# Gated linear attention with a cosine-gated feed-forward behind it: 256-token units, a second product that is held back, decay groups of two chunks, and elementwise products on GpSimd

## The chip, the cores and the metric

The kernel runs on one core of one Trainium2 chip. The metric is the time of one execution on the device in microseconds. The kernel before was timed in three runs: median 227.28 us (226.5 to 227.76). One execution was profiled; it took 227.1 us, of which the trace spans 225.3 us from the first to the last instruction.

## The reference, cut to what matters

There are 4 sequences of 768 tokens with 8 heads of 48 channels. The first stage is a gated linear recurrence for each head; its output, laid out as 3072 tokens of 384 channels, goes into a feed-forward stage with two products.

```
f = 1 / (1 + exp(-f_logit))
for t in range(768):
    state = f[:, :, t, :, None] * state + k[:, :, t] (outer) v[:, :, t]
    y[:, :, t] = q[:, :, t] @ state
x = y.transpose(0, 2, 1, 3).reshape(3072, 384)
h = x @ w_in            # 384 x 2048
out = (h * cos(h)) @ w_out   # 2048 x 384
```

Inputs and the output are float32. Matmul operands are bfloat16 in the kernel.

## The kernel before, in words

**Attention by chunks.** Each sequence is cut into 6 chunks of 128 tokens, so there are 24 chunks, numbered 0 to 23 here. `chunk_load` brings f, v, k and q of a chunk (192 KB each) on the SP queue; six sets of load buffers rotate. `decay_group` (L313 on) takes a group of chunks: on ScalarE exp and ln of f (L328, L331) give the log decay, TensorE sums it over the tokens with a triangular matrix (L343, L346), and ScalarE makes exp of the sum and of its negative (L353: `b` and `bi`). `attend` then multiplies q by `b` and k by `bi` (L365 and L368, `qtd` and `ktd`, each on VectorE or GpSimd), GpSimd casts v (L371, `vz`), TensorE transposes both (L383), ScalarE or VectorE copies the result from PSUM (L397 or L399, `qdt` and `kz`), TensorE forms the scores (L414), VectorE masks them (L419, `am`), TensorE forms the output of the chunk (L481 from the scores, L485 from the state), and ScalarE or VectorE casts it to `xT` (L496 or L498). Beside this the state goes on from chunk to chunk: L434 on TensorE, L445 on VectorE (`st`), L453 on GpSimd (`sz`).

**Feed-forward by units.** `moe(t0, T)` takes a unit of T tokens: four units of 128 and then five of 512. The first product (L516) fills a PSUM bank of 512 columns at a time (a tile); ScalarE takes the cosine of it (L523), VectorE multiplies the two into `gT` (L527; `gc` in the small units). The second product (L537) is issued in steps of four matmuls, sixteen for 128 tokens; the result is copied (L546 or L548) and stored by the SP queue (L551). There are 8 PSUM banks; the tiles of the first product hold at most 4, and both products together at most 5.

**Two sets of function tables.** exp and ln are in one table set of ScalarE and the cosine (computed as a sine) is in another. Going from one to the other costs an ACT_TABLE_LOAD (L582 for exp and ln, L523 for the sine). Copies and casts need neither. From the first exp of a decay group to its last, ScalarE takes no cosine.

**What sets the order.** All instructions are first written down as operations with a cost, an engine or a choice of engines, a priority `prio` and their inputs and outputs. `Plan.run` then sets them one by one: of all operations whose inputs are set it takes the one that can start first by the costs, and of those with the same start the one with the lowest `prio`. The resulting order is fixed; on the chip each engine works through its own list and waits where an input or a buffer is not there. For attention `prio` is the chunk number; for the feed-forward it is 2.0 plus the first chunk of the unit plus a part for the tile. `GROUPS` gives the sizes of the decay groups: 1, 1, 1, 1, 2, and then six times 3.

Of the kernel before, what the change touches and what calls it, by code (L numbers as in the profile page):

```python
# [207 lines left out]
def kernel(  # L208
# [11 lines left out]
    B, H, S, D = q.shape  # L220
    C = 128
# [5 lines left out]
    KF = d_ff // 128  # L227
    TOK = 512
    NT = n_tokens // TOK
    GROUPS = [1, 1, 1, 1, 2] + [3] * 6  # L230
    LEAD = 2.0

    cpool = ctx.enter_context(tc.tile_pool(name="const", bufs=1))
    ppool = ctx.enter_context(tc.tile_pool(name="psum", bufs=1, space=bass.MemoryType.PSUM))
# [6 lines left out]
    def slots(name, n, shape, dt=BF16, zero=None):  # L241
        aps = []
        for i in range(n):
            t = cpool.tile(shape, dt, name=f"{name}_{i}")
            if zero is not None:
                zero.memset(t, 0.0)
            aps.append(t)
        return Slots(aps, name)
# [20 lines left out]
    szS = slots("sz", 3, [128, NP, SW], zero=nc.vector)  # L269
    stS = slots("st", 2, [128, NP, 2 * D], F32)  # L270
    x_sb = [cpool.tile([128, KM, TOK], BF16, name=f"xT_{i}") for i in range(NT)]
    gS = slots("gT", 2, [128, KF, TOK])
    gcS = slots("gc", 4, [128, KF, C])
    coS = slots("cosh", 4, [128, TOK])
    otS = slots("ot", 4, [128, d_model], F32)
    base = banks("ps", 8)
# [8 lines left out]
    P = Plan()  # L285
# [7 lines left out]
    def load_weights(part, i, prio):  # L293
# [3 lines left out]
        else:  # L297
# [7 lines left out]
    xT = [Val(ap=x_sb[n * C // TOK][:, :, n * C % TOK:n * C % TOK + C])  # L305
          for n in range(n_tokens // C)]
# [13 lines left out]
    def decay_group(chunks, g, prio):  # L320

        outs = []
        for (b, c, ld) in chunks:
# [8 lines left out]

            e1 = P.op({"ACT": 515.0}, act1, reads=[f], writes=[f], prio=prio, table="E", grp=g)
            P.op({"ACT": 515.0}, act2, reads=[f], writes=[sp], prio=prio, table="E", grp=g)
            for (_, _, ld2) in chunks:
# [3 lines left out]
        for (b, c, ld, sp) in outs:  # L339
# [12 lines left out]
            def ex(e, pc=pc, o=bt, s=-1.0, n=H * D + NP):  # L352
                nc.scalar.activation(out=o.ap, in_=pc.ap[:, 0:n], func=AF.Exp, scale=s)  # L353

            P.op({"ACT": 400.0}, ex, reads=[pc], writes=[bt], prio=prio, table="E", grp=g)
            P.op({"ACT": 400.0}, lambda e, pc=pc, bi=bi, ex=ex: ex(e, pc, bi, 1.0, H * D),
                 reads=[pc], writes=[bi], prio=prio, table="E", grp=g)
            res.append((b, c, ld, bt, bi))
        return res

    def attend(b, c, ld, bt, bi, prio):
        _, vf, kf, qf = ld
        qtd, ktd, vz = Val(qtdS), Val(ktdS), Val(vzS)
        E = lambda e: nc.vector if e == "DVE" else nc.gpsimd
        P.op({"POOL": 1000.0, "DVE": 560.0}, lambda e: E(e).tensor_mul(  # L365
            out=qtd.ap[:, :, 0:D], in0=qf.ap,
            in1=bt.ap[:, 0:H * D].rearrange("p (h d) -> p h d", d=D)), reads=[qf, bt], writes=[qtd], prio=prio)
        P.op({"POOL": 1000.0, "DVE": 560.0}, lambda e: E(e).tensor_mul(  # L368
            out=ktd.ap[:, :, 0:D], in0=kf.ap,
            in1=bi.ap.rearrange("p (h d) -> p h d", d=D)), reads=[kf, bi], writes=[ktd], prio=prio)  # L370
        o = P.op({"POOL": 510.0}, lambda e: nc.gpsimd.tensor_copy(  # L371
# [114 lines left out]
                                     rhs=qdt.ap[:, n, :], **fl)  # L486
        rd = [vz, qdt] + ams + ([S_in] if S_in is not None else [])
        P.op({"PE": len(jobs) * N128}, pey, reads=rd, writes=[py], prio=prio, lat=170.0)
        tok = b * S + c * C
        x = xT[tok // C]  # L490

        def yev(e):
# [9 lines left out]
    def moe(t0, T):  # L502

        n0 = t0 // C
        xs, gT = xT[n0:(t0 + T) // C], Val(gS if T == TOK else gcS)
        x = x_sb[t0 // TOK][:, :, t0 % TOK:t0 % TOK + T]
        G = 512 // T
        span = T / C
        for j in range(KF // G):
            ph, co = Val(phS), Val(coS)  # L510

            def g1(e, j=j, ph=ph):
                for g in range(G):
                    f0 = (j * G + g) * 128
                    for m in range(KM):
                        nc.tensor.matmul(ph.ap[:, g * T:(g + 1) * T],  # L516
                                         lhsT=w_in_bf[:, m, f0:f0 + 128], rhs=x[:, m, :],
                                         start=(g == 0 and m == 0),
                                         stop=(g == G - 1 and m == KM - 1))
            pr = LEAD + n0 + 0.5 * span * j * G / KF  # L520
            P.op({"PE": G * 3 * (T / 2.4 + 2.0)}, g1, reads=xs + [w_in_v[j * G // 4]],
                 writes=[ph], prio=pr, lat=170.0)
            P.op({"ACT": 640.0}, lambda e, ph=ph, co=co: nc.scalar.activation(  # L523
                out=co.ap, in_=ph.ap, func=AF.Sin, bias=halfpi),
                reads=[ph], writes=[co], prio=pr, table="S")
            gv = gT.part(lambda a, j=j: a[:, j * G:(j + 1) * G, 0:T])
            P.op({"DVE": 650.0}, lambda e, ph=ph, co=co, gv=gv: nc.vector.tensor_mul(  # L527
                out=gv.ap, in0=ph.ap.rearrange("p (g t) -> p g t", t=T),
                in1=co.ap.rearrange("p (g t) -> p g t", t=T)),
                reads=[ph, co], writes=[gv], prio=pr)  # L530
        for i in range(T // 128):
            po, ot = Val(poS), Val(otS)
            pr = LEAD + n0 + 0.5 * span + 0.5 * i
            for s in range(4):
                def g2(e, i=i, s=s, po=po):
                    for j in range(4 * s, 4 * s + 4):
                        nc.tensor.matmul(po.ap[:, 0:d_model],  # L537
                                         lhsT=gT.ap[:, j, i * 128:(i + 1) * 128],
                                         rhs=w_out_bf[:, j, :], start=(j == 0), stop=(j == KF - 1))
                P.op({"PE": 4 * 162.5}, g2,  # L540
                     reads=[gT.parts[q] for q in range(4 * s // G, (4 * s + 3) // G + 1)] + [w_out_v[s]],
                     writes=[po], prio=pr, lat=170.0 if s == 3 else 0.0)

            def ev(e, po=po, ot=ot):
                if e == "ACT":
                    nc.scalar.copy(out=ot.ap, in_=po.ap[:, 0:d_model])  # L546
                else:
                    nc.vector.tensor_copy(out=ot.ap, in_=po.ap[:, 0:d_model])  # L548
            P.op({"ACT": 380.0, "DVE": 530.0}, ev, reads=[po], writes=[ot], prio=pr)
            r0 = t0 + i * 128  # L550
            P.op({"SP": 500.0}, lambda e, ot=ot, r0=r0: nc.sync.dma_start(  # L551
                out=out[r0:r0 + 128, :], in_=ot.ap), reads=[ot], prio=pr, lat=2000.0)
# [2 lines left out]
    nc.vector.memset(halfpi, HALF_PI)  # L555

    chunks = [(b, c) for b in range(B) for c in range(NCH)]
    units = [C] * (TOK // C) + [TOK] * (NT - 1)
    n, t0 = 0, 0
    for g, size in enumerate(GROUPS):  # L560
        grp = []
        for j, (b, c) in enumerate(chunks[n:n + size]):
            grp.append((b, c, chunk_load(b, c, float(n + j))))
        for j, item in enumerate(decay_group(grp, g, float(n))):
            attend(*item, prio=float(n + j))
            if n + j == 0:
                for i in range(NW):
                    load_weights(0, i, 0.2 + 0.1 * i)
                for i in range(KF // 4):
                    load_weights(1, i, 1.2 + 0.5 * i)  # L570
        n += size
        while units and t0 + units[0] <= n * C:
            moe(t0, units[0])
            t0 += units.pop(0)
# [40 lines left out]
```

## Time and profile before

| | us |
|---|---|
| median of 3 runs (lowest, highest) | 227.28 (226.5, 227.76) |
| the profiled execution | 227.1 |
| its span in the trace | 225.3 |
| TensorE (PE) busy | 192.8 (86%) |
| ScalarE (ACT) busy | 159.6 (71%) |
| VectorE (DVE) busy | 151.1 (67%) |
| GpSimd (POOL) busy | 52.3 (23%) |
| mean granted TensorE clock | 0.975 |

Busy time is the time in which at least one instruction of the engine was under way; the end of a matmul is modelled, so a row of matmuls is best priced by the distance between starts. The chain of waits is followed back from the last instruction; its rows give a start, a duration and what was under way, and "issue" is time in which nothing that the profile shows was waited for. PEld is the loading of weights, which overlaps matmuls. HBM transfers use 1.0 of the DMA engines' time up to about 120 us, when the last inputs have come, and little after it.

### The profile page before, as it was taken

What the parts mean: (1) busy time and instruction counts of PE and PEld (TensorE: products, weight loads), DVE (VectorE), ACT (ScalarE), POOL (GpSimd) and SP (SyncE); (2) the same over time, 40 slices, a digit from 0 to 9 for tenths busy, and PEclk for the clock granted to TensorE, in tenths of its full rate; (3) what the DMA queues carried; (4) which work ended last, traced back from release to release, by engine and by line L of the source; (5) the groups of instructions that cost most, each with busy time, mean ns of one, the idle gap of its engine ahead of it and who ended that gap; (6) DMA issues with size and microseconds to landing.
All of it is one profiled execution on the core that took longest, in us unless ns stands there. A gap on an engine that the chain in (4) does not pass through costs nothing.

```text
span 225.3 us, 4647 instructions
## 1 busy us (share of the span) xinstructions
PE 192.8 (86%) x1760; PEld 128.2 (57%) x1760; DVE 151.1 (67%) x269; ACT 159.6 (71%) x283; POOL 52.3 (23%) x86
## 2 busy tenths in 40 slices
PE   0076788998579889999969999999999999889994
PEld 0056466877369445676743567645676456654562
DVE  7854647788396499449997934998069971449800
ACT  4237559999886999748695984999569962449721
POOL 3800503212034430118380030600038000300000
PEclk9999999999967999999996999999999999999998
DMA  6999998999999999498999212000110001100011
GB/s 137 185 187 185 172 193 186 198 205 204 193 206 212 183 225 186 115 214 168 207 210 210 40 70 73 0 0 3 70 73 3 0 3 70 70 3 0 0 70 70
DMA packets 107030, 27.03 MB, mean 120 GB/s; under 512 B 100353, under 2 KB 107009, under 8 KB 107009
## 3 DMA queue, kind: packets, MB, share of 16 engines
q1 hardware_dynamic: 103296, 23.60, 49.7%
q0 software_dynamic: 3712, 3.15, 8.8%
q8 instruction: 13, 0.21, 0.4%
q14 instruction: 9, 0.07, 0.1%
HBM read 25.17 MB, written 4.72 MB: 133 GB/s over the span
## 4 chain that ended last, share of the span: by engine, by line
PE 66%; DVE 13%; ACT 10%; issue 6%; POOL 2%; DVEq 0%; POOLq 0%
PE ps L537 26%; PE ps L516 25%; PE ps L481 5%; PE ps L414 4%; PE ps L383 3%; ACT kz L397 3%; DVE am L419 2%; PE ps L485 2%; DVE ktd L368 2%; DVE qtd L365 1%; DVE gc L527 1%; ACT L523 1%; ACT bi L353 1%; ACT b L353 1%; ACT xT L496 1%
## 5 line engine op out<-in xcount | busy, mean ns | idle before, releaser
L516 PE MATMUL ps<-xT,w_in_bf 128*128 128x512 bf16 (+1 forms) x432 | 67.8, 316 | 3.0 <-ACT xT L496 1.4
L523 ACT ACTIVATE cosh<-ps,halfpi 128x512 bf16<-128x512 f32 x96 | 60.2, 697 | 4.1 <-PE ps L516 4.0
L537 PE MATMUL ps<-w_out_bf,gT 128*128 128x384 bf16 x320 | 53.6, 326 | 0.0
L516 PEld LDWEIGHTS <-w_in_bf 128*128 128x128 bf16 x432 | 35.7, 101 | 31.3 <-issue 5.9
L527 DVE TENSOR_TENSOR gT<-ps,cosh 128x512 bf16<-128x512 f32 x80 | 50.1, 686 | 4.7 <-ACT cosh L523 4.7
L419 DVE TENSOR_TENSOR am<-ps,umask 128x512 bf16<-128x512 f32 x48 | 30.6, 684 | 27.2 <-PE ps L414 26.4
L537 PEld LDWEIGHTS <-gT 128*128 128x128 bf16 x320 | 31.1, 98 | 20.6
L453 POOL TENSOR_TENSOR sz<-st,b 64x192 bf16<-64x192 f32 x32 | 16.6, 519 | 83.4 <-DVE st L445 78.7
L546 ACT COPY ot<-ps 128x384 f32<-128x384 f32 x17 | 8.2, 479 | 24.5 <-PE ps L537 24.5
L371 POOL CAST vz<-v 128x384 bf16<-128x384 f32 x24 | 13.5, 563 | 47.6 <-PE ps L481 20.1
L481 PE MATMUL ps<-am,vz 128*128 128x128 bf16 x240 | 23.2, 226 | 0.7 <-DVE am L419 0.6
L414 PE MATMUL ps<-qdt,kz 128*128 128x128 bf16 x192 | 18.7, 233 | 5.2 <-ACT kz L397 4.0
L397 ACT COPY kz<-ps 64x512 bf16<-64x512 bf16 x26 | 15.1, 580 | 10.2 <-DVE qdt L399 8.0
L481 PEld LDWEIGHTS <-vz 128*128 128x128 bf16 x240 | 17.5, 101 | 2.5 <-issue 1.1
L414 PEld LDWEIGHTS <-kz 128*128 128x128 bf16 x192 | 13.4, 104 | 9.6 <-ACT kz L397 6.4
L496 ACT CAST xT<-ps 128x384 bf16<-128x384 f32 x18 | 8.7, 484 | 13.9 <-PE ps L485 10.3
L365 DVE TENSOR_TENSOR qtd<-q,b 128x384 bf16<-128x384 f32 x16 | 10.3, 648 | 10.9 <-ACT b L353 10.8
L383 PE MATMUL ps<-ident,qtd 128*128 128x128 bf16 x96 | 10.0, 230 | 8.7 <-DVE qtd L365 8.1
L485 PE MATMUL ps<-qdt,sz 128*128 128x128 bf16 x120 | 16.5, 219 | 0.0
L353 ACT ACTIVATE b<-ps 128x388 f32<-128x388 f32 x24 | 12.0, 499 | 5.1 <-PE ps L346 5.0
L368 DVE TENSOR_TENSOR ktd<-k,bi 128x384 bf16<-128x384 f32 x18 | 14.1, 788 | 0.4 <-ACT bi L353 0.2
L343 PE MATMUL ps<-sp,umask 128*128 128x384 bf16 x24 | 8.0, 339 | 7.4 <-ACT sp L331 7.4
(43 smaller groups left out, 216.8 us busy)
## 6 DMA issues: line engine op xcount, KB each, us to landing
f<-in_f_logit_dram SPq DMA_DIRECT2D x24, 192.0 KB, 3.7
v<-in_v_dram SPq DMA_DIRECT2D x24, 192.0 KB, 3.6
k<-in_k_dram SPq DMA_DIRECT2D x24, 192.0 KB, 3.7
q<-in_q_dram SPq DMA_DIRECT2D x24, 192.0 KB, 3.8
out_dram<-ot SPq DMA_DIRECT2D x24, 192.0 KB, 1.8
w_in_bf<-in_moe_w_in_dram POOLq DMA_DIRECT2D x4, 384.0 KB, 9.1
w_out_bf<-in_moe_w_out_dram POOLq DMA_DIRECT2D x4, 384.0 KB, 11.1
```

What stands on the lines that cost most here:

```text
L368: P.op({"POOL": 1000.0, "DVE": 560.0}, lambda e: E(e).tensor_mul(out=ktd.ap[:, :, 0:D], in0=kf.ap, in1=bi.ap.rearrange("p (h d) -> p h d", ...
L383: nc.tensor.transpose(out=o[:, j + p, :], in_=t.ap[:, 2 * p:2 * p + 2, :].rearrange("p h d -> p (h d)"), identity=ident)
L397: nc.scalar.copy(out=d, in_=s)
L414: nc.tensor.matmul(o[:, i, :], lhsT=kz.ap[:, h // 2, h % 2, :], rhs=qdt.ap[:, h // 2, :], start=(i == 0), stop=(i == 3))
L419: nc.vector.tensor_mul(out=am.ap, in0=pa.ap.rearrange("p (a n) -> p a n", n=C), in1=umask[:, None, :].broadcast_to([128, 4, C]))
L453: eng.tensor_mul(out=S_out.ap[r, :, 128 + par * D:128 + par * D + D], in0=srcap()[r, :, par * D:par * D + D], in1=bt.ap[r, H * D:, None].b ...
L481: nc.tensor.matmul(o[:, t, :], lhsT=vz.ap[:, w0:w0 + 128], rhs=ams[n // 4].ap[:, n % 4, :], **fl)
L485: nc.tensor.matmul(o[:, t, :], lhsT=S_in.ap[:, n, w0:w0 + 128], rhs=qdt.ap[:, n, :], **fl)
L516: nc.tensor.matmul(ph.ap[:, g * T:(g + 1) * T], lhsT=w_in_bf[:, m, f0:f0 + 128], rhs=x[:, m, :], start=(g == 0 and m == 0), stop=(g == G - ...
L523: P.op({"ACT": 640.0}, lambda e, ph=ph, co=co: nc.scalar.activation(out=co.ap, in_=ph.ap, func=AF.Sin, bias=halfpi), reads=[ph], writes=[c ...
L527: P.op({"DVE": 650.0}, lambda e, ph=ph, co=co, gv=gv: nc.vector.tensor_mul(out=gv.ap, in0=ph.ap.rearrange("p (g t) -> p g t", t=T), in1=co ...
L537: nc.tensor.matmul(po.ap[:, 0:d_model], lhsT=gT.ap[:, j, i * 128:(i + 1) * 128], rhs=w_out_bf[:, j, :], start=(j == 0), stop=(j == KF - 1))
```

## The change

The list of decay groups, the list of units and three constants change; the first unit of each kind has its own `gT` buffers, four of 128 tokens and four of 256 in place of four of 128 and two of 512. The second product gets `LAG` = 5.0 added to its `prio`, so that among operations that can start at the same time it comes behind the attention of up to five later chunks and behind the first product of later units. From the third chunk on, `qtd` and `ktd` may go to GpSimd only.

```diff
-    GROUPS = [1, 1, 1, 1, 2] + [3] * 6
-    LEAD = 2.0
+    GROUPS = [1] * 4 + [2] * 10
+    FAST, LAG = 2, 5.0
+    LEAD, RATE = 2.0, 1.0
+    UNITS = [128] * 4 + [256] * 10
+    GT_BUFS = {128: 4, 256: 4}
...
-    gS = slots("gT", 2, [128, KF, TOK])
-    gcS = slots("gc", 4, [128, KF, C])
+    gS = {T: slots(f"gT{T}", n, [128, KF, T]) for T, n in GT_BUFS.items()}
...
+        tok = b * S + c * C
         qtd, ktd, vz = Val(qtdS), Val(ktdS), Val(vzS)
+        ew = {"POOL": 1000.0, "DVE": 560.0} if tok < FAST * C else {"POOL": 1000.0}
         E = lambda e: nc.vector if e == "DVE" else nc.gpsimd
-        P.op({"POOL": 1000.0, "DVE": 560.0}, lambda e: E(e).tensor_mul(
+        P.op(dict(ew), lambda e: E(e).tensor_mul(
...
-            pr = LEAD + n0 + 0.5 * span * j * G / KF
+            pr = LEAD + RATE * n0 + 0.5 * span * j * G / KF
...
-            pr = LEAD + n0 + 0.5 * span + 0.5 * i
+            pr = LEAD + LAG + RATE * n0 + 0.5 * span + 0.5 * i
...
-    units = [C] * (TOK // C) + [TOK] * (NT - 1)
+    units = list(UNITS)
```

The first four decay groups and the order of the first two chunks are the same. On ScalarE, the next rows are those at the end of the decay group that begins with chunk 6 (chunks 6 to 8), in the kernel before: `b` and `bi` are L353, `qdt` and `kz` are the copies of the transposes, f is the exp of the next group.

```order
L353 ACTIVATE b_106<-ps_176 128x388
L353 ACTIVATE bi_111<-ps_176 128x384
L397 COPY qdt_132<-ps_175 128x512
L397 COPY kz_135<-ps_175 64x4x128
L397 COPY qdt_133<-ps_177 128x512
L397 COPY kz_137<-ps_177 64x4x128 x2
L397 COPY qdt_134<-ps_180 128x512
L397 COPY kz_139<-ps_180 64x4x128 x2
L496 CAST xT_154<-ps_174 128x3x128
L496 CAST xT_154<-ps_178 128x3x128
L328 ACTIVATE f_74<-f_74 128x384
L328 ACTIVATE f_75<-f_75 128x384
```

The same engine and place in the changed kernel (here the group is chunks 6 and 7), whose numbers of lines are 2 to 4 higher (L355 for L353, L526 for L523, L585 for L582):

```order
L355 ACTIVATE b_108<-ps_179 128x388
L355 ACTIVATE bi_110<-ps_179 128x384
L526 ACT_TABLE_LOAD
L526 ACTIVATE cosh_167<-ps_180,halfpi 128x512
L401 COPY kz_135<-ps_177 64x4x128
L526 ACTIVATE cosh_168<-ps_181,halfpi 128x512
L526 ACTIVATE cosh_169<-ps_182,halfpi 128x512
L526 ACTIVATE cosh_170<-ps_178,halfpi 128x512
L526 ACTIVATE cosh_167<-ps_179,halfpi 128x512
L401 COPY qdt_133<-ps_180 128x512
L585 ACT_TABLE_LOAD
L330 ACTIVATE f_73<-f_73 128x384
```

Before, two groups of three follow one another under one table, and no cosine stands between them; now a table load, five cosines and another table load stand between two groups of two. In the whole program there are 13 loads of each table in place of 8.

On TensorE the scores of chunk 6 stand so in the kernel before (the matmuls with `kz` are L414, those with `ident` the transposes of chunk 8):

```order
L414 MATMUL ps_174<-qdt_132,kz_135 128x128
L414 LDWEIGHTS kz_135
L414 MATMUL ps_173<-qdt_132,kz_135 128x128
...
L383 LDWEIGHTS qtd_116
L383 MATMUL ps_180<-ident,qtd_116 128x128
```

and so in the changed kernel (L418 for L414, L540 for L537, the second product, L519 for L516, the first one):

```order
L418 MATMUL ps_177<-qdt_132,kz_135 128x128
L540 LDWEIGHTS gT_3_162
L540 MATMUL ps_176<-w_out_bf,gT_3_162 128x384
...
L418 LDWEIGHTS kz_135
L418 MATMUL ps_181<-qdt_132,kz_135 128x128
...
L519 LDWEIGHTS w_in_bf
L519 MATMUL ps_177<-xT_154,w_in_bf 128x256
```

Four matmuls of the second product (each with its weights) now stand between the two halves of the scores, and the first product follows in tiles of six matmuls of 256 columns. Counted through the order at the place where L343 (now L345) sums the decay of a chunk, the matmuls of the second product whose first product has been issued, and that are not issued themselves, are 0 to 16 before; now they are 8 at chunk 6, 28 at chunk 8, 44 at chunk 14, and 60 at chunk 23. Behind the last first product stand 64 before and 84 now.

On GpSimd, the kernel before has these rows about the `qtd` of chunk 8:

```order
L371 CAST vz_126<-v_92 128x8x48
L365 TENSOR_TENSOR qtd_116<-q_85,b_106 128x8x48
L453 TENSOR_TENSOR sz_145<-st_151,b_108 64x4x48
L371 CAST vz_128<-v_93 128x8x48
L453 TENSOR_TENSOR sz_145<-st_151,b_108 64x4x48
L453 TENSOR_TENSOR sz_147<-st_152,b_106 64x4x48
```

and the changed kernel these about the group of chunks 4 and 5 (L369 and L372 are the products, L375 the cast, L457 the state):

```order
L375 CAST vz_126<-v_94 128x8x48
L457 TENSOR_TENSOR sz_145<-st_151,b_108 64x4x48
L369 TENSOR_TENSOR qtd_114<-q_87,b_105 128x8x48
L372 TENSOR_TENSOR ktd_120<-k_81,bi_110 128x8x48
L369 TENSOR_TENSOR qtd_116<-q_88,b_106 128x8x48
L372 TENSOR_TENSOR ktd_122<-k_82,bi_111 128x8x48
```

The four products of a group now stand in one row on GpSimd, with the state and the casts ahead of or behind them. Of the 48 products, 14 were on GpSimd before and 44 are now.

## Rows read from the trace of the kernel before

**Rows 1.** The page: busy us of each engine, share of span, instructions.
```profile
PE 192.8 (86%) x1760; PEld 128.2 (57%) x1760; DVE 151.1 (67%) x269; ACT 159.6 (71%) x283; POOL 52.3 (23%) x86
```

**Rows 2.** Stretches, us: length; busy PE, PEld, DVE, ACT, POOL; PEclk, DMA, GB/s.
```profile
57.80:225.30 167.50, 153.12 (x1273) 96.51 (x1271) 109.91 (x187) 121.32 (x222) 36.67 (x54) 0.97 0.44 97
...
119.70:201.10 81.40, 78.81 (x637) 48.76 (x636) 53.34 (x90) 59.69 (x106) 14.60 (x22) 0.99 0.15 44
...
27.90:57.80 29.90, 27.16 (x362) 21.76 (x360) 22.54 (x42) 24.63 (x40) 5.88 (x12) 1.00 1.01 198
...
114.00:118.00 4.00, 2.09 (x29) 1.43 (x26) 4.00 (x7) 3.97 (x7) 3.62 (x4) 1.00 1.04 207
118.00:122.00 4.00, 3.83 (x10) 1.41 (x10) 3.08 (x6) 1.58 (x4) 0.00 (x0) 0.57 1.05 210
```

**Rows 3.** The chain of waits in order of time: start us, us, what.
```profile
39.75 1.34 PE ps L516 x24
...
57.80 1.28 ACT L582
...
74.41 3.20 issue
...
80.29 7.77 PE ps L516 x36
...
118.17 9.62 PE ps L516 x36
...
201.12 10.52 PE ps L516 x48
211.64 10.41 PE ps L537 x64
222.08 0.48 ACT ot L546
```

**Rows 4.** The timeline of PE: start us, us, instruction and count.
```profile
139.62 0.33 PE L343 MATMUL ps<-sp,umask 128*128 128x384 bf16 x1
...
139.89 0.33 PE L481 MATMUL ps<-am,vz 128*128 128x128 bf16 x3
...
140.78 0.33 PE L343 MATMUL ps<-sp,umask 128*128 128x384 bf16 x1
...
164.79 0.61 PE L414 MATMUL ps<-qdt,kz 128*128 128x128 bf16 x8
165.24 0.39 PE L383 MATMUL ps<-ident,qtd 128*128 128x128 bf16 x4
...
165.69 0.33 PE L434 MATMUL ps<-vz,ktd 128*128 128x96 bf16 x4
165.86 0.39 PE L383 MATMUL ps<-ident,qtd 128*128 128x128 bf16 x4
```

**Rows 5.** Groups of ACT by shape: count, busy us, mean ns, idle before.
```profile
L582 ACT ACT_TABLE_LOAD x8 | 10.3, 1283 | 0.9 <-PEq L599 0.7
L523 ACT ACT_TABLE_LOAD x8 | 10.3, 1283 | 0.1
...
L496 ACT CAST xT<-ps 128x384 bf16<-128x384 f32 x18 | 8.7, 484 | 13.9 <-PE ps L485 10.3 <-PE ps L481 3.6
...
L546 ACT COPY ot<-ps 128x384 f32<-128x384 f32 x17 | 8.2, 479 | 24.5 <-PE ps L537 24.5
```

**Rows 6.** Groups of `qtd` and `ktd`, DVE and POOL, by shape.
```profile
L368 DVE TENSOR_TENSOR ktd<-k,bi 128x384 bf16<-128x384 f32 x18 | 14.1, 788 | 0.4 <-ACT bi L353 0.2
...
L365 DVE TENSOR_TENSOR qtd<-q,b 128x384 bf16<-128x384 f32 x16 | 10.3, 648 | 10.9 <-ACT b L353 10.8
...
L365 POOL TENSOR_TENSOR qtd<-q,b 128x384 bf16<-128x384 f32 x8 | 8.7, 1092 | 12.9 <-issue 7.8 <-ACT b L353 3.5 <-DMA f<-in_f_logit_dram 1.5
...
L368 POOL TENSOR_TENSOR ktd<-k,bi 128x384 bf16<-128x384 f32 x6 | 7.0, 1169 | 0.4 <-ACT bi L353 0.4
```

**Rows 7.** The timeline of ACT and DVE around chunk 2.
```profile
30.59 0.49 ACT L353 ACTIVATE b<-ps 128x388 f32<-128x388 f32 x1 [2.94 <-PE ps L346]
...
31.12 0.56 DVE L365 TENSOR_TENSOR qtd<-q,b 128x384 bf16<-128x384 f32 x1 [2.36 <-ACT b L353]
...
31.59 0.55 DVE L368 TENSOR_TENSOR ktd<-k,bi 128x384 bf16<-128x384 f32 x1
```

More of the change, by code (lines that the diff above doesn't have):

```diff
@@ L362, in attend @@
         _, vf, kf, qf = ld
+        tok = b * S + c * C
         qtd, ktd, vz = Val(qtdS), Val(ktdS), Val(vzS)
+        ew = {"POOL": 1000.0, "DVE": 560.0} if tok < FAST * C else {"POOL": 1000.0}
         E = lambda e: nc.vector if e == "DVE" else nc.gpsimd
-        P.op({"POOL": 1000.0, "DVE": 560.0}, lambda e: E(e).tensor_mul(
+        P.op(dict(ew), lambda e: E(e).tensor_mul(
             out=qtd.ap[:, :, 0:D], in0=qf.ap,
             in1=bt.ap[:, 0:H * D].rearrange("p (h d) -> p h d", d=D)), reads=[qf, bt], writes=[qtd], prio=prio)
-        P.op({"POOL": 1000.0, "DVE": 560.0}, lambda e: E(e).tensor_mul(
+        P.op(dict(ew), lambda e: E(e).tensor_mul(
             out=ktd.ap[:, :, 0:D], in0=kf.ap,
@@ L488, in attend @@
         P.op({"PE": len(jobs) * N128}, pey, reads=rd, writes=[py], prio=prio, lat=170.0)
-        tok = b * S + c * C
         x = xT[tok // C]
@@ L504, in moe @@
         n0 = t0 // C
-        xs, gT = xT[n0:(t0 + T) // C], Val(gS if T == TOK else gcS)
+        xs, gT = xT[n0:(t0 + T) // C], Val(gS[T])
         x = x_sb[t0 // TOK][:, :, t0 % TOK:t0 % TOK + T]
```

## The prediction
> **What bounds the kernel now.** I read the shares of the engines first: TensorE is busy 86% of the span, ScalarE 71%, GpSimd 23% [rows 1]. An average over the span hides stages, so the windows come next. From 57.8 us on TensorE is busy 153.1 of 167.5 us, and from 119.7 to 201.1 us it is busy 78.8 of 81.4 us, or 97%, while ScalarE has 73% there [rows 2]. That is TensorE's stage. From 27.9 to 57.8 us, with groups of one chunk and units of 128 tokens, ScalarE is busy 24.6 of 29.9 us, which is 82%, and the DMA engines are full.
>
> The chain of waits shows where TensorE lost time behind 57.8 us [rows 3]. At 57.8 a table load begins the group of chunks 6 to 8; the first tile of 512 columns that runs freely starts at 80.3, at 118.2 there is another such block, at 201.1 the last one. Between these, piece by piece, I set the work in the order against the time.
>
> Prices of TensorE's work, from the distance between starts. A second product: 64 matmuls in 10.41 us, 162.7 ns each. A first product of 512 columns: 36 in 7.77 us, 216 ns; of 128 columns: 24 in 1.34 us, 56 ns [rows 3]. The attention of a chunk: scores 0.45 us, transposes 0.45 (164.79 to 165.24 to 165.69), state 0.17 (165.69 to 165.86), sum of the decay 0.27 (139.62 to 139.89), output 0.89 (139.89 to 140.78) [rows 4]; together 2.23 us. The 18 chunks left at 57.8 us need 18 x 2.23 = 40.1, less 1.5 since three of them open a sequence (ten matmuls of output rather than sixteen) and three close one (no state): 38.6. The first product needs 240 x 216 ns = 51.8, the second 320 matmuls and 4 that were under way, 52.7. The sum is 143.1 us, done in 222.1 - 57.8 = 164.3 us: 87%, and 21.2 us are lost. By the order and these prices, 57.8 to 80.3 holds 12.1 us of work in 22.5 (10.4 lost: the table of the exponentials stays loaded for six chunks, no cosine can be made, and no feed-forward is left to do); 80.3 to 118.2 holds 33.2 in 37.9 (4.7 lost); 118.2 to 201.1 holds 77.2 in 82.9 (5.7 lost). Of the last, 1.85 us are one block of 36 matmuls that took 9.62 us where the same block took 7.77 [rows 3]; the granted clock was 0.57 from 118 to 122 us, so at the lower level of 1.2 GHz for most of it, after a stretch in which TensorE was busy 2.09 of 4 us [rows 2].
>
> **The change part by part.** *The reserve.* The second product is held behind attention and first products, so 8 to 60 of its matmuls (1.3 to 9.8 us) can fill any hole, where 0 to 16 stood before. It adds no work. At the end 84 rather than 64 of them stand behind the last first product: 84 x 162.7 ns = 13.7 us, against 10.4; but the last first product is 48 matmuls of half the width, 5.2 us, against 10.5. The stretch that only the last unit can fill shrinks from 20.9 to 18.9 us, and it runs without loss, since 64 matmuls after one another took what they cost.
>
> *Units of 256.* 480 matmuls of 256 columns replace 240 of 512. The trace has no such matmul; two of 128 columns (112 ns) and half of one of 512 (108 ns) bound it, so 51.8 to 53.8 us. I take 109 ns, near the wider one: 52.3 us, or 0.5 more. Weight loads double in number; at 56 ns a matmul of 128 columns already came with a weight load each, so they hide. TensorE's work behind 57.8 us is then 38.6 + 52.3 + 328 x 162.7 ns (53.4) = 144.3 us.
>
> *Groups of two.* The order has 18 table loads behind the point where 8 stood. Each took 1283 ns [rows 5], so ScalarE gets 12.8 us. Seven casts of `xT` go to VectorE, 7 x 0.484 = 3.4 us; other copies stay in number. ScalarE's 121.3 us behind 57.8 us [rows 2] become 121.3 + 12.8 - 3.4 = 130.7. Six output copies of 0.479 us come behind the last cosine, so 127.8 us have to be done before it. Nothing hides a part of this if TensorE has no reserve; with it, up to 9.8 us of a ScalarE lag are covered.
>
> The Trainium skill speaks against this part: "ScalarE: Activation LUTs", section "Table sets: the hidden batching unit", says to do all calls of one table set before going to the next, and its example prices a load at about 2.7 us. The trace has 1.283 us, so the measurement decides; at 2.7 us the 18 loads and the 8 that they replace would differ by 27 us, ScalarE would have 142 us to do by that estimate, and the gain below would be gone.
>
> *Products on GpSimd.* Of 48 products, 44 are on GpSimd in place of 14. They take 1.09 and 1.17 us there, 0.65 and 0.79 on VectorE [rows 6]; VectorE loses 30 of them, 14 x 0.648 + 16 x 0.788 = 21.7 us, and was no bound. GpSimd gets at most 30 x 1.17 = 35 us more behind 57.8 us, some 72 us in 155. What waits is the chain: chunk 2 had `b` at 30.59, `qtd` at 31.12 and `ktd` at 31.59 on VectorE [rows 7], 0.5 us apart. On GpSimd each takes some 1.1, so the transposes come 1.0 to 1.3 us later for each of chunks 2 to 5, ahead of the reserve's growth. Queued behind a product on GpSimd are the state update and the cast of v, and TensorE waits for those. Ends: 0 (hidden by the second product, 4 matmuls of which now stand there) and 4 x 1.3 = 5.2 us. I take 1.0, near the covered end, because first products also stand between. From chunk 6 on the reserve covers it.
>
> **The sum.** The last output needs 225.3 - 222.05 = 3.25 us behind the last matmul, as before. With e the share of time in which TensorE works between 58.8 us (57.8 and the 1.0) and the last unit, the span is 58.8 + (144.3 - 18.9)/e + 18.9 + 3.25. For e I take the longest stretch in which TensorE had work in stock, 118.2 to 201.1, without the 1.85 us of lower clock: 77.2/81.1 = 0.95. That gives 58.8 + 132.0 + 22.2 = 213.0. The profiled execution took 227.1 for a span of 225.3, so 1.8 us lie around it: **214.8, say 215 us**; this execution is 0.2 us under the median of 227.28. ScalarE would have to do 127.8 us in 213.0 - 16.0 - 58.8 = 138.2 us, 92% (16.0 being 12.8 us of second product behind the last cosine and 3.25). No long stretch of the trace has that; this is the weak point, and the rivals stand on it.
>
> **Rivals.** *The reserve fills all:* e = 1 gives 58.8 - 1.0 + 125.4 + 22.2 = 205.4, and 207.2 with the 1.8. For it: 97% busy at 119.7 to 201.1. Against: ScalarE would need 127.8 in 131.6 us.
>
> *The ratio of the early stage stays:* TensorE worked from 27.9 to 57.8 us on 26.0 us of work (by the order) in 29.9, 0.87, with the same kind of fine interleaving. 58.8 + 125.4/0.87 + 22.2 = 225.1, and 226.9 in all: no change. For it: that stretch is the nearest in its form. Against: it had no reserve, and 2.94 us of ScalarE's idle time in it was one wait for the start of chunk 2 [rows 7].
>
> *ScalarE becomes the bound, and the kernel slower:* each group locks out the cosine for two table loads and two chunks of exponentials, and between the sp and the `b` of each group ScalarE waits for its matmul to come up in TensorE's list. If its busy share stays at the early stage's 24.63/29.9 = 0.82, the span is 58.8 + 127.8/0.82 + 16.0 = 230.7, and the time 232.5. It decides below 127.8/(225.3 - 16.0 - 58.8) = 0.85. For it: 0.82 was the highest share in any long window. Against: ScalarE waited there for TensorE as well, which now has what to do when ScalarE is late.
>
> *The change does not do what it says:* the low rank counts only among operations that can start together; but the order does hold 8 to 84 matmuls back, so only its use is open, and that is the second rival.
>
> **How the numbers follow.** My forecast of 215 with 210 to 221 about it has 0.52, the full fill 0.15, the early ratio 0.17, the slower ScalarE 0.14, and 0.02 is left for other things. A difference under 0.5% cannot be told from none, so faster means under 226.1 and slower over 228.4. Faster: 0.52 + 0.15 + a half of the early ratio, 0.76. Same: 0.09. Slower: 0.15. The range goes from the full fill, 207, to 228, past the early ratio; it leaves out most of the slower case.
>
> **What would show it.** Right: in the windows behind 58 us TensorE at 93% or more, ScalarE near 90% until the last cosine, 26 table loads, no stretch without cosines beyond 8 us, no half clock; the chain of waits mostly on the two products, the last first product ending some 17 us ahead of the end. The products on GpSimd at 1.0 to 1.2 us. Wrong: waits of TensorE for ScalarE's `kz` and `xT` or for GpSimd's `ktd` in every group, which sum to over 10 us; a chain through table loads and exponentials; `qtd` and `ktd` well above 1.2 us; or chunk 6 starting more than 3 us later than 57.8.

## The result, and the profile after

The changed kernel takes 211.56 us, the median of four runs (210.29 to 211.9), where four runs of the kernel before (the three of the first table and one more) have a median of 227.52 us (226.5 to 228.39). The ratio is 0.929, with a 95% interval of 0.9234 to 0.9346. The forecast was 215 us with a range of 207 to 228. The profiled execution took 211.75 us for a span of 209.6 us; the spans differ by 15.7 us.

The page of the changed kernel, busy us of each engine, share of the span and instructions, against [rows 1]:

```profile
PE 187.2 (89%) x2000; PEld 149.8 (71%) x2000; DVE 135.1 (64%) x247; ACT 166.3 (79%) x285; POOL 77.3 (37%) x116
```

The shares rose for TensorE, ScalarE and GpSimd, but the average still hides the stage that matters. The windows of the changed kernel, with the columns of [rows 2]:

```profile
27.90:57.80 29.90, 26.52 (x353) 21.23 (x352) 16.45 (x31) 25.51 (x42) 13.25 (x20) 1.00 1.06 202
57.80:178.00 120.20, 119.29 (x1319) 98.28 (x1317) 89.80 (x162) 114.43 (x201) 54.15 (x76) 1.00 0.57 122
57.80:193.40 135.60, 134.69 (x1461) 110.55 (x1459) 100.22 (x178) 125.25 (x220) 54.49 (x76) 1.00 0.51 111
57.80:209.60 151.80, 147.58 (x1539) 118.08 (x1536) 100.91 (x179) 128.04 (x225) 54.49 (x76) 1.00 0.48 107
```

In the stretch from 27.9 to 57.8 us TensorE is about as busy as before (26.52 us against 27.16 [rows 2]); VectorE has 6.1 us less to do there and GpSimd 7.4 us more. Behind 57.8 us TensorE is busy 119.29 of 120.2 us, or 99%, with a granted clock of 1.00 all the way, and ScalarE 114.43, or 95%. The same stretch of the kernel before:

```profile
57.80:178.00 120.20, 111.02 (x980) 71.96 (x979) 87.84 (x152) 97.49 (x182) 34.66 (x50) 0.96 0.57 122
```

So ScalarE did 17 us more work in those 120 us, and TensorE was busy 8 us more.

The mean clock of 0.96 before is a loss of another kind. Beside the stretch at 118 us that the prediction named, TensorE worked at the lower level of 1.2 GHz for most of 64 to 72 us, after it had been busy 2.94 of 6.2 us.

```profile
57.80:64.00 6.20, 2.94 (x34) 1.86 (x33) 2.65 (x5) 6.19 (x14) 1.38 (x3) 0.98 0.91 190
64.00:72.00 8.00, 7.34 (x82) 6.93 (x81) 6.92 (x13) 5.04 (x10) 2.17 (x4) 0.59 1.07 211
```

```profile
65.86 1.14 PE L414 MATMUL ps<-qdt,kz 128*128 128x128 bf16 x8
...
70.65 0.33 PE L481 MATMUL ps<-am,vz 128*128 128x128 bf16 x3
```

From 65.86 to 70.65 us TensorE had no pause and took 4.79 us for three blocks of scores, the transposes and the state of one chunk, and ten matmuls of output. At the prediction's prices these are 2.53 us, so 2.3 us went to the clock. The prediction counted 1.85 us of this kind, at 118 us, and put all of the 10.4 us lost up to 80.3 us down to missing work.

Where TensorE's idle time went is read from the view of waits, which lists what an engine waited for, us in total, times and the longest. All that TensorE waited for between 57.8 and 178 us in the changed kernel:

```profile
PE ps L519 <- DVE am L423: 0.2, 1, 0.2
PE ps L485 <- DVE am L423: 0.2, 1, 0.2
PE ps L540 <- ACT bi L355: 0.2, 1, 0.2
```

and the four longest of the kernel before:

```profile
PE ps L343 <- ACT sp L331: 2.7, 2, 1.9
PE ps L383 <- DVE ktd L368: 2.1, 4, 0.9
PE ps L383 <- DVE qtd L365: 1.1, 3, 0.7
PE ps L516 <- DVE gT L527: 0.9, 1, 0.9
```

Before, TensorE stood in front of the sum of a decay group or of transposes until ScalarE or VectorE had their operands ready. After, 0.6 us of waits are left in 120 us.

The groups of TensorE's instructions under way between 57.80 and 187.40 us, where the last unit's 48 first products begin in the chain of waits, give the work by count:

```profile
L519 PE MATMUL ps<-xT,w_in_bf 128*128 128x256 bf16 x434 | 52.9, 273 | 0.4 <-DVE am L423 0.2
L540 PE MATMUL ps<-w_out_bf,gT 128*128 128x384 bf16 x248 | 47.5, 326 | 0.3 <-ACT bi L355 0.2
L485 PE MATMUL ps<-am,vz 128*128 128x128 bf16 x191 | 17.7, 219 | 0.2 <-DVE am L423 0.2
L489 PE MATMUL ps<-qdt,sz 128*128 128x128 bf16 x98 | 13.5, 219 | 0.0
```

The view also counts what reaches over an end of the stretch: two of the last unit's first products, and three matmuls of output that began before 57.80. Without these it is 432 x 109 ns = 47.1 us, 248 x 162.7 ns = 40.3 us and, at an output's 0.89 us for sixteen matmuls, 286 x 55.6 ns = 15.9 us; scores, transposes, state and sums of 18 chunks add 23.6 us. That is 126.9 us of work in 129.6 us, or 98%. The end of the chain of waits (start us, us, what), against the last rows of [rows 3]:

```profile
187.40 5.24 PE ps L519 x48
192.64 13.66 PE ps L540 x84
```

Behind 57.8 us TensorE lost 21.2 us before (143.1 us of work in 164.3). Now it has 126.9 + 18.9 = 145.8 us of work and takes 206.3 - 57.8 = 148.5, so it loses 2.7. That is 18.5 us of loss less and 2.7 us of work more, and the difference is 15.8 us, as in the spans. Of the 21.2 us before, 11.2 were idle (164.3 less the 153.12 busy of [rows 2]) and some 4 were the lower clock; the rest, some 6 us, is not told apart here.

### The profile page after: what moved, and what is told of

It is laid out like the page before. It is cut to its first block, busy times and chain, and to the rows that moved or that the text cites. A ratio compares the mean times of both kernels' runs of the same rounds, so it can differ in the third digit from the quotient of the medians.

```text
span 209.6 us, 5117 instructions
## 1 busy us (share of the span) xinstructions
PE 187.2 (89%) x2000; PEld 149.8 (71%) x2000; DVE 135.1 (64%) x247; ACT 166.3 (79%) x285; POOL 77.3 (37%) x116
## 4 chain that ended last, share of the span: by engine, by line
PE 72%; DVE 13%; ACT 8%; issue 4%; POOL 0%; DVEq 0%; ACTq 0%; POOLq 0%
PE ps L540 27%; PE ps L519 25%; PE ps L485 6%; PE ps L387 4%; PE ps L418 4%; PE ps L489 3%; DVE gT L530 3%; ACT cosh L526 2%; DVE am L423 2%; ACT L526 1%; ACT kz L401 1%; PE ps L345 1%; DVE kz L403 1%; DVE vz L249 1%; PE ps L438 1%
## 5 line engine op out<-in xcount | busy, mean ns | idle before, releaser
L530 DVE TENSOR_TENSOR gT<-ps,cosh 128x512 bf16<-128x512 f32 x96 | 61.8, 683 | 18.4 <-ACT cosh L526 18.1
L519 PE MATMUL ps<-xT,w_in_bf 128*128 128x256 bf16 (+1 forms) x672 | 71.4, 262 | 1.9 <-ACT xT L499 0.9
L540 PE MATMUL ps<-w_out_bf,gT 128*128 128x384 bf16 x384 | 72.1, 328 | 1.1 <-DVE gT L530 0.8
L519 PEld LDWEIGHTS <-w_in_bf 128*128 128x128 bf16 x672 | 58.7, 100 | 8.4 <-issue 2.2
L526 ACT ACTIVATE cosh<-ps,halfpi 128x512 bf16<-128x512 f32 x96 | 60.1, 691 | 3.4 <-PE ps L519 3.1
L540 PEld LDWEIGHTS <-gT 128*128 128x128 bf16 x384 | 35.3, 98 | 20.0 <-DVE gT L530 1.3
L457 POOL TENSOR_TENSOR sz<-st,b 64x192 bf16<-64x192 f32 x32 | 16.1, 502 | 44.7 <-DVE st L449 40.0
L369 POOL TENSOR_TENSOR qtd<-q,b 128x384 bf16<-128x384 f32 x22 | 21.9, 997 | 22.1 <-ACT b L355 14.0
L375 POOL CAST vz<-v 128x384 bf16<-128x384 f32 x24 | 12.1, 505 | 33.6 <-PE ps L485 18.5
L401 ACT COPY kz<-ps 64x512 bf16<-64x512 bf16 x28 | 16.4, 584 | 8.1 <-DVE qdt L403 7.9
L372 POOL TENSOR_TENSOR ktd<-k,bi 128x384 bf16<-128x384 f32 x22 | 21.9, 998 | 0.0
L418 PE MATMUL ps<-qdt,kz 128*128 128x128 bf16 x192 | 17.3, 227 | 2.0 <-DVE kz L403 1.0
L418 PEld LDWEIGHTS <-kz 128*128 128x128 bf16 x192 | 13.2, 101 | 5.7 <-DVE kz L403 1.8
L355 ACT ACTIVATE b<-ps 128x388 f32<-128x388 f32 x24 | 11.9, 498 | 5.9 <-PE ps L348 5.1
```

What stands on the lines that cost most here:

```text
L369: P.op(dict(ew), lambda e: E(e).tensor_mul(out=qtd.ap[:, :, 0:D], in0=qf.ap, in1=bt.ap[:, 0:H * D].rearrange("p (h d) -> p h d", d=D)), re ...
L372: P.op(dict(ew), lambda e: E(e).tensor_mul(out=ktd.ap[:, :, 0:D], in0=kf.ap, in1=bi.ap.rearrange("p (h d) -> p h d", d=D)), reads=[kf, bi] ...
L401: nc.scalar.copy(out=d, in_=s)
L418: nc.tensor.matmul(o[:, i, :], lhsT=kz.ap[:, h // 2, h % 2, :], rhs=qdt.ap[:, h // 2, :], start=(i == 0), stop=(i == 3))
L519: nc.tensor.matmul(ph.ap[:, g * T:(g + 1) * T], lhsT=w_in_bf[:, m, f0:f0 + 128], rhs=x[:, m, :], start=(g == 0 and m == 0), stop=(g == G - ...
L540: nc.tensor.matmul(po.ap[:, 0:d_model], lhsT=gT.ap[:, j, i * 128:(i + 1) * 128], rhs=w_out_bf[:, j, :], start=(j == 0), stop=(j == KF - 1))
```

## The experiments

The expectations weigh two theories. By the first, called A in the first of them, the held-back second product is what counts, since it gives TensorE something to do whenever ScalarE is late. By its rival, B, the shorter units and groups do it, since they leave no long hole. The later expectations say for themselves what each theory is. Every change below is against the changed kernel, unless it says otherwise, and every ratio is against the kernel before, run beside it.

**No reserve.** Everything of the change stays, but the second product is not held back.

```diff
-    FAST, LAG = 2, 5.0
+    FAST, LAG = 2, 0.0
```

> The changed kernel with LAG at 0, so that the second product is not held back; its order keeps 4 to 20 second products in stock rather than 8 to 60, and 32 stand behind the last first product. Theory A (the held-back product fills the holes, and is what the change is worth): most of the gain goes, 220 to 226 us. Theory B (the short units and groups alone end the long stretch without a cosine, and the holding back adds little): 212 to 215 us.

Measured: 231.2 us (230.02 to 231.41), ratio 1.0221 (1.0143 to 1.0298), which is 19.6 us above the changed kernel and slower than the kernel before. It lies beyond both figures, and on the side of A. The windows and ScalarE's waits of this run:

```profile
57.80:178.00 120.20, 108.74 (x1135) 85.31 (x1134) 77.39 (x139) 96.27 (x171) 47.66 (x66) 1.00 0.58 124
```

```profile
ACT xT L499 <- PE ps L489: 10.0, 4, 3.1
ACT xT L499 <- PE ps L485: 6.2, 2, 3.1
ACT b L355 <- PE ps L348: 2.9, 3, 1.8
```

In the changed kernel the same three waits are

```profile
ACT xT L499 <- PE ps L489: 1.9, 2, 1.3
ACT b L355 <- PE ps L348: 0.7, 1, 0.7
...
ACT xT L499 <- PE ps L485: 0.2, 1, 0.2
```

and the chain of waits of the run without the reserve shows what ScalarE waited behind:

```profile
108.98 5.20 PE ps L540 x32
...
114.83 0.45 PE ps L418 x8
...
118.69 0.09 PE ps L348 x4
...
118.87 0.50 ACT b L355
```

The second product of a unit of 256 tokens stands there as one lump of 32 matmuls, 5.2 us, ahead of the scores, the outputs and the sum of the decay. ScalarE, which has its casts and its next exponentials behind those, is idle for up to 3.1 us, and its share falls to 80%. What it does not do then is missing from TensorE later. So the low rank of the second product does two things: it gives TensorE stock, and it lets what ScalarE needs go first. As a gain the prediction had only the first; ScalarE's wait for its matmul stands in it in the slower rival.

**The reserve alone,** in the kernel before, with its units of 512 and groups of three.

```diff
-            pr = LEAD + n0 + 0.5 * span + 0.5 * i
+            pr = LEAD + 5.0 + n0 + 0.5 * span + 0.5 * i
```

> The kernel before with the 5.0 added to the rank of its second product and nothing else. Its order has no second product in stock at chunks 6 to 8 (the stretch from 58 to 80 us), 16 to 56 later, and 96 at the end. Theory A: 212 to 217 us. Theory B: the 10.4 us lost from 57.8 to 80.3 stay, and a part of the other 10.5 goes: 220 to 227 us.

Measured: 223.6 us (223.19 to 225.54), ratio 0.9898 (0.9819 to 0.9976), a gain of 2 to 3 us of the 16 (by the ratio, by the medians). From 57.8 to 80 us TensorE has hardly more to do than before; this run is the first line, the kernel before, at its lower clock, the second:

```profile
57.80:80.00 22.20, 15.55 (x185) 10.82 (x184) 14.82 (x29) 19.68 (x42) 8.71 (x13) 1.00 0.96 197
...
57.80:80.00 22.20, 16.57 (x179) 12.77 (x178) 13.48 (x26) 18.86 (x39) 7.87 (x13) 0.85 0.99 198
```

There no second product is pending in this order: the units of 128 are done, and the first unit of 512 has to wait for chunk 7. A rank cannot hold back what does not exist. Neither theory alone gives the result: short units and groups without the rank lose 4.7 us against the kernel before, the rank without them gains 2 to 3, and both together gain 16.

**Groups of three, the rest as changed.**

```diff
-    GROUPS = [1] * 4 + [2] * 10
+    GROUPS = [1, 1, 1, 1, 2] + [3] * 6
```

> The changed kernel with the decay groups of the kernel before (1, 1, 1, 1, 2, six times 3): 20 table loads rather than 26, 7.7 us less for ScalarE, longer stretches without a cosine. If ScalarE's table loads hold the changed kernel back: 208 to 211 us. If the size of the groups does not matter with a stock: 211 to 213 us. If short groups are what opened the stretch from 58 to 80 us: 216 to 222 us.

Measured: 216.04 us (215.5 to 217.07), ratio 0.9552 (0.9485 to 0.9619). The six table loads that this saves (20 in place of 26) do not pay: it is 4.5 us slower than groups of two. From 80 to 120 us TensorE has 3.2 us of holes, where the changed kernel (second line) has 0.1. The longest waits in them stand below:

```profile
80.00:120.00 40.00, 36.82 (x410) 29.97 (x408) 30.43 (x56) 36.70 (x67) 17.55 (x24) 1.00 0.84 172
...
80.00:120.00 40.00, 39.94 (x442) 33.07 (x440) 30.09 (x54) 37.59 (x66) 17.49 (x24) 1.00 0.95 199
```

```profile
PE ps L387 <- POOL ktd L372: 1.7, 3, 0.6
...
PE ps L387 <- POOL qtd L369: 0.7, 2, 0.4
```

So 2.4 of the 3.2 us are waits for products on GpSimd, which has six of them for a group of three. A run of groups of three with products on both engines was not made, so how much of the 4.5 us comes from the longer stretches without a cosine is not shown.

**Units of 512, the rest as changed.**

```diff
-    UNITS = [128] * 4 + [256] * 10
-    GT_BUFS = {128: 4, 256: 4}
+    UNITS = [128] * 4 + [512] * 5
+    GT_BUFS = {128: 4, 512: 2}
```

> The changed kernel with units of 512 tokens behind the first four (two buffers of gT for them): 16 table loads by its order, stock 0 at chunks 8 and 9. If the width of the unit does not matter once the second product is held back: 211 to 214 us. If a unit of 512 comes too late to fill the stretch behind chunk 6 (it needs four chunks of xT): TensorE loses 5 to 8 us there again, 216 to 221 us.

Measured: 215.28 us (214.52 to 216.49), ratio 0.9518 (0.9448 to 0.9588), 3.7 us above the changed kernel. That is between the two ranges of the expectation. The loss is where the first unit of 512 is still to come, and the granted clock falls there; in the same two stretches the changed kernel has TensorE busy for 5.98 and 7.79 us, at 1.00:

```profile
57.80:64.00 6.20, 4.60 (x53) 2.93 (x51) 3.27 (x8) 5.59 (x15) 4.09 (x5) 1.00 0.91 188
64.00:72.00 8.00, 7.25 (x88) 6.00 (x87) 5.95 (x11) 5.55 (x12) 5.61 (x8) 0.79 1.06 221
```

**Products on both engines,** as they were before the change.

```diff
-    FAST, LAG = 2, 5.0
+    FAST, LAG = 24, 5.0
```

> The changed kernel with FAST at 24, so that every qtd and ktd may go to VectorE or GpSimd, whichever the order finds first. If the 1.0 us products on GpSimd lie off the path thanks to the stock: 210 to 213 us. If their length costs something in each group: 206 to 209 us. If VectorE, freed of them, is what let the tiles of the feed-forward run on: 214 to 219 us.

Measured: 212.0 us (211.86 to 212.29), ratio 0.9293 (0.9214 to 0.9371). That is the time of the changed kernel. The products did move: GpSimd was busy 31 us rather than 54 from 57.8 to 178 us, VectorE 103 rather than 90. So in the time of the whole kernel this part of the change is worth nothing, in either direction. In the profiled executions two small differences cancel: this run has TensorE busy 117.84 of the 120.2 us, where the changed kernel has 119.29, but it comes to 57.8 us with 1.7 us less work left (5 matmuls of the second product and 16 of outputs), at a granted clock of 1.00 from 22 to 30 us where the changed kernel had 0.79.

**A smaller reserve.**

```diff
-    FAST, LAG = 2, 5.0
+    FAST, LAG = 2, 2.0
```

> The changed kernel with LAG at 2.0: by its order 16 to 36 second products in stock, 52 at the end. If what counts is that attention and the sum of the decay go ahead of the second product, and not how much is in stock: 211 to 215 us. If the depth of the stock counts: 217 to 225 us, between 211.6 and the 231 without any LAG.

Measured: 219.44 us (218.81 to 219.59), ratio 0.9612 (0.9544 to 0.9679). With a lag of 0, 2 and 5 chunks the time is 231.2, 219.4 and 211.6 us. By the expectation this says that the depth of the stock counts, and not only that attention goes first. The window of this run lies between the two others:

```profile
57.80:178.00 120.20, 113.51 (x1221) 91.02 (x1219) 75.62 (x136) 107.66 (x194) 48.78 (x68) 1.00 0.60 128
```

More lag than 5 was not tried.

**Which engine is the limit now: half of the second product.** Of the 16 matmuls of each sum, 8 are left out, so half of the terms of the second product are missing; all else stands in the same places.

```diff
-                    for j in range(4 * s, 4 * s + 4):
+                    for j in (4 * s, 4 * s + 3):
```

> The changed kernel with only two of four matmuls in each step of the second product (half of the output's sum is left out), in the same order: 192 x 162.7 ns = 31.2 us less for TensorE, 6.8 of it behind the last first product. If TensorE alone bounds the changed kernel: 180 to 185 us. If ScalarE stands right behind it and can be pressed to nearly full use: 194 to 199 us. If ScalarE at its 92% is the bound already, only the end gets shorter: 203 to 206 us.

Measured: 197.11 us (196.75 to 199.7), ratio 0.8663 (0.8576 to 0.8749). TensorE has 192 x 162.7 ns = 31.2 us less to do, and the time falls by 14.5 us, of which 6.8 are in the tail (42 matmuls in place of 84). In the stretch before it ScalarE takes over as the limit, with 98%:

```profile
57.80:178.00 120.20, 112.68 (x1264) 92.05 (x1262) 94.51 (x170) 117.98 (x210) 54.08 (x76) 1.00 0.57 123
```

**More work on ScalarE.** `b` and `bi` are computed twice each, in the same order.

```diff
-                nc.scalar.activation(out=o.ap, in_=pc.ap[:, 0:n], func=AF.Exp, scale=s)
+                for _ in range(2):
+                    nc.scalar.activation(out=o.ap, in_=pc.ap[:, 0:n], func=AF.Exp, scale=s)
```

> The changed kernel with each of the exponentials b and bi computed twice into the same place, in the same order: 48 more activations of 0.39 us, 18.7 us more for ScalarE, 14.0 of them behind 58 us. If ScalarE has the rest of its time as slack and TensorE is the bound: 213 to 218 us. If its share of 92% cannot rise: 224 to 229 us.

Measured: 231.63 us (230.98 to 232.52), ratio 1.0146 (1.0053 to 1.024). This is beyond both ranges of the expectation: an exponential more took 0.475 us and not 0.39. ScalarE's busy time on the page goes from 166.3 to 189.1 us, by 22.8, and the time by 20.1:

```profile
57.80:178.00 120.20, 107.53 (x1156) 85.50 (x1156) 79.66 (x144) 115.89 (x208) 47.80 (x67) 1.00 0.56 120
```

ScalarE has 96% here and TensorE 89%, and the kernel is slower than the one before. This is the prediction's slower rival, ScalarE as the bound, brought about on purpose: of 22.8 us that ScalarE is given, 20.1 are paid. That `b` and `bi` themselves come later is a small part of it: TensorE's waits for `bi` in this stretch sum to 2.7 us, those for `gT`, which needs the cosine, to 6.3.

**Less work on ScalarE.** The copies of the transposes (`qdt`, `kz`) go to VectorE only.

```diff
-        both = {"DVE": 425.0, "ACT": 500.0}
+        both = {"DVE": 425.0}
```

> The changed kernel with the copies qdt and kz on VectorE only: 41 of 0.58 us leave ScalarE, seven casts of xT and five output copies come to it, two table loads fewer, so some 18 us less there; VectorE gets some 10 us more. Its order has 48 to 80 second products in stock from chunk 10 on. If ScalarE's load is what keeps TensorE from working without a gap: 206 to 209 us (the floor by TensorE's work was 207.2). If TensorE is the only bound already: 210 to 212 us. If VectorE comes into the way with all three copies in a row: 213 to 218 us.

Measured: 211.2 us (211.07 to 214.19), ratio 0.9353 (0.9219 to 0.9488): no difference from the changed kernel.

```profile
57.80:178.00 120.20, 117.88 (x1316) 98.10 (x1314) 95.79 (x183) 98.84 (x171) 52.72 (x75) 1.00 0.56 120
```

ScalarE has 15.6 us less to do there and falls to 82%, TensorE stays at 98%, and the time stays. TensorE is the limit of the changed kernel, and ScalarE is just under it. Taken together, the two runs say that the distance between them is small: more on ScalarE costs at once, less gains nothing.

**The first microseconds.** The chain of the changed kernel begins with zeroing buffers on VectorE. Eight of these are kept ahead and thirteen go to GpSimd behind its first `w_out` load.

```diff
-    spS = slots("sp", 5, [128, H, 64], zero=nc.vector)
+    spS = slots("sp", 5, [128, H, 64], zero=nc.vector, first=2)
...
+            if o is last_w:
+                for t in later:
+                    nc.gpsimd.memset(t, 0.0)
```

> The changed kernel, where VectorE zeroes only the buffers that the first two chunks need (8 memsets, some 3.8 us, in place of 21 and 9.1 us) and GpSimd the other 13 behind the first part of w_out; the first qtd can start 5 us sooner. If the rest of the program simply moves ahead: 206 to 208 us. If the loads of chunks and weights set the pace up to 58 us: 210 to 212 us. If GpSimd's memsets hold up the weights or the cast of v: 213 us or more.

Measured: 210.76 us (210.19 to 212.01), ratio 0.9321 (0.9194 to 0.9448), which cannot be told from the changed kernel. VectorE is busy 13.3 us rather than 17.8 in the first 27.9 us, but the chain now begins elsewhere, with the load of the first weights:

```profile
7.73 11.83 DMA w_in_bf<-in_moe_w_in_dram
```

With the zeroing out of the way, TensorE waits for weights that land at 19.6 us. In this execution the granted clock from 18 to 26 us was also only 0.58, where the changed kernel's was 0.90; what the weights and what the clock took of the earlier start is not separated.

**Both of the last two.** The edit is that of the two runs above together.

> Both of these edits together. If their gains add up: 201 to 205 us. If the early stage is bound by loads: as with the copies alone.

Measured: 211.44 us (211.3 to 212.67), ratio 0.9344 (0.9247 to 0.9442). Its chain goes through GpSimd's zeroing, from 9.2 to 19.4 us, and a load of `w_out`; the four second products behind it took 1.44 us at 26.65, where four cost 0.65. No version that ran and does all of the work is measurably better than the changed kernel.

## Why the prediction was right

**The mechanism was right.** TensorE lost 21.2 us behind 57.8 us, and the reserve takes away all but 2.7 of them. The windows, the waits and the three lags show it. The prediction had the long holes and put too little down to the clock: with the holes the 2.3 us of half clock at 65.86 us went too. Shorter groups, so that cosines do not stop for long, were in its account of the stretch from 57.8 to 80.3 us; that shorter units give stock early was not. The runs with groups of three and units of 512 price the two at 4.5 and 3.7 us by the medians (5.9 and 5.2 by the ratios, 0.026 and 0.023 of 227.5), the first with the waits for GpSimd in it.

**The mis-sized term is e,** the share of time in which TensorE works up to the last unit. The prediction took 0.95 from the best stretch of before; measured is 126.9/129.6 = 0.98, nearer to the rival's 1 than to the forecast's 0.95. At 0.95 the 126.9 us would have taken 133.6, so this step is off by 4.0 us. ScalarE's share, the weak point, is 125.25/135.6 = 92% from 57.8 to 193.4 us, as forecast, and it was reached with waits of a few us in all.

**The early delay** was put at 1.0 us. At 57.8 us there were 1.5 us more work left than the prediction counted: 4 more matmuls of the second product and 16 more of outputs. At 0.95 that is 1.6 us in place of 1.0, 0.6 more. The two errors, -4.0 and +0.6, are the 3.4 us by which the span of 209.6 us lies under the forecast of 213.0.

The cause given for this term, products on GpSimd, did not make it; that its size came near is chance. In the changed kernel `b` of chunk 2 comes 1.3 us later than in [rows 7], before GpSimd has had any product:

```profile
31.93 0.49 ACT L355 ACTIVATE b<-ps 128x388 f32<-128x388 f32 x1 [3.10 <-PE ps L348]
```

Up to there TensorE ran slower in this execution: the first 48 first products behind 17.50 us took 4.48 us, against 3.70 before, and the granted clock from 22 to 30 us was 0.79, against 1.00. The windows of the changed kernel, of the kernel before and of the run with groups of three:

```profile
22.00:30.00 8.00, 5.33 (x44) 3.73 (x45) 5.29 (x10) 3.61 (x6) 2.95 (x5) 0.79 0.95 159
...
22.00:30.00 8.00, 5.37 (x66) 4.00 (x67) 4.68 (x9) 2.91 (x4) 2.95 (x5) 1.00 1.06 172
...
22.00:30.00 8.00, 5.48 (x68) 4.12 (x69) 4.57 (x9) 2.91 (x4) 2.94 (x5) 1.00 1.09 177
```

The run with groups of three has the same groups up to chunk 5 and the same products on GpSimd. There `b` of chunk 2 comes at 30.48 us, and at 57.8 us 328 matmuls of the second product and 271 of outputs are still to start, against the 328 and 270 that the prediction counted. So in that run the products on GpSimd cost nothing up to there.

**The prices** held. A block of 48 first products of 256 columns took 5.24 us, 109.2 ns each, where 109 was taken. The stretch of the last unit was forecast at 18.9 us and took 5.24 + 13.66 = 18.90; the last output needs 3.3 us against 3.25. ScalarE was forecast at 130.7 us behind 57.8 and has 128.0; 0.7 of the difference is a table load that begins at 57.13. Behind 58 us the granted clock is 1.00 throughout. The longest stretch without a cosine is 8.8 us, a little over the 8 that were named, where 27.0 stood before. There are 26 table loads at the price of [rows 5]:

```profile
L585 ACT ACT_TABLE_LOAD x13 | 16.7, 1283 | 0.9 <-PEq L602 0.7
L526 ACT ACT_TABLE_LOAD x13 | 16.7, 1283 | 0.2
```

On these the Trainium skill, "ScalarE: Activation LUTs", section "Table sets: the hidden batching unit", says to batch activation calls by set. Fewer changes of set did not help here: the kernel with 26 loads takes 211.56 us and the one with 20, in groups of three, 216.04, though the waits for GpSimd are a part of that difference.

**The rivals.** The ratio of the early stage (226.9 us) did not come back: that stage still has 26.52 of 29.9 us, and the later one has a stock that it lacks. ScalarE as the bound (232.5 us) did not come about in the changed kernel, but it was one edit away: with 22.8 us more on ScalarE the time is 231.63. The share of 0.82 that this rival feared is what the kernel shows without the reserve (0.80, 231.2 us). So its chance hung on the order, and the prediction's reason against it, that ScalarE had waited for TensorE, was the right one.

What stays open: the first 57.8 us, in which TensorE is busy 39.6 us, did not yield to moving the zeroing, and the weights, the loads of the inputs and the lower clock in some executions were not separated.

## What to carry to other kernels

Where two engines feed each other and both are over 90% busy, the order between them can be worth more than the work, as it was here: put first on the busier engine what the other waits for, and hold back work that nobody waits for, in pieces small enough to fill a hole. Such a rank needs stock, so the units behind it must be short enough that there is some early, and more table changes can be the cheaper choice if they keep the stock coming. To see which engine is the limit, add work to one and take work from it: cost in full one way and no gain the other way mean that it stands just under the bound.

## What the hardware showed that was not expected

The products on VectorE and GpSimd are slow where they meet; on VectorE also beside GpSimd's cast of v (0.86 us at 96.19 us of the run with products on both engines). With the products on GpSimd alone, each takes the same time, and the four on VectorE at the start take 0.55 us each. The groups by shape of the changed kernel (engine, operation, count, busy us, mean ns), against means of 648 and 788 ns on VectorE and 1092 and 1169 on GpSimd in [rows 6]:

```profile
L369 POOL TENSOR_TENSOR qtd<-q,b 128x384 bf16<-128x384 f32 x22 | 21.9, 997 | 22.1 <-ACT b L355 14.0
L372 POOL TENSOR_TENSOR ktd<-k,bi 128x384 bf16<-128x384 f32 x22 | 21.9, 998 | 0.0
...
L369 DVE TENSOR_TENSOR qtd<-q,b 128x384 bf16<-128x384 f32 x2 | 1.1, 552 | 0.0
```

With products on both engines, the timelines of VectorE and of GpSimd show some that meet:

```profile
112.94 1.83 DVE L369 TENSOR_TENSOR qtd<-q,b 128x384 bf16<-128x384 f32 x2
```

```profile
113.21 1.13 POOL L372 TENSOR_TENSOR ktd<-k,bi 128x384 bf16<-128x384 f32 x1 [1.43 <-ACT bi L355]
```

Two products of VectorE that alone take 1.1 us take 1.83 beside one of GpSimd, which takes 1.13 in place of 1.00. The Trainium skill, "SBUF — State Buffer", section "SBUF: two separate sides", describes it as a lock: of a VectorE operation with two inputs in SBUF and a GpSimd operation that reads SBUF, the one that starts later waits for the other to end. The trace agrees with it to within 0.2 us: had each waited for the end of the other engine's, GpSimd's product would have ended at 114.49 us and VectorE's second at 114.89; they ended at 114.34 and 114.77.
